# Pooled attention and two feed-forward layers: later three-pass products in block 0, an account of conversion buffers, and other buffers for the last output tiles

## The chip, the cores and the metric

One core of one Trainium2 chip runs the kernel. The metric is the device time of one launch in microseconds (us). The engines are TensorE (PE; its weight loads stand as PEld), VectorE (DVE), ScalarE (ACT), GpSimd (POOL) and SyncE (SP, which issues all the transfers).

## The reference

```python
def _attn_ref(q, k, v):              # 4 batches, 8 heads, 576 tokens, head size 64
    k_p = k.reshape(B, H, Sp, 8, D).mean(axis=3)
    v_p = v.reshape(B, H, Sp, 8, D).mean(axis=3)
    attn = softmax(q @ k_p^T / sqrt(D))
    return attn @ v_p
def _moe_ref(x, w_in, w_out):        # 2304 x 512, 512 x 2048, 2048 x 512
    h = x @ w_in
    g = where(h >= 1, h, where(h <= -1, 0, (h + 1) ** 2 / 4))
    return g @ w_out
def _moe2_ref(x, w_in, w_out):       # the same shapes
    h = x @ w_in
    g = maximum(h, 0) + log1p(exp(-abs(h)))
    return g @ w_out
out = _moe2_ref(_moe_ref(rows of _attn_ref, w_in, w_out), w_in2, w_out2)
```

All is float32. The softmax and the reshapes are abbreviated here.

## The kernel before

The weights come in as 64-bit words. A *conversion* turns a tile of them into float32: two ACT passes (`words`, L112), three DVE passes (`exponents`, L119), a product and a sum. A product in float32 is either made *whole*, one matmul on float32 operands, or in *three passes* on operands split into a high part and a rest in FP32R: high x high, high x rest, rest x high. A split takes an ACT copy (the high part) and a DVE subtraction (the rest).

**Stage 1** is attention and the first feed-forward layer. The 18 tiles of 128 tokens are cut into five blocks of 4, 4, 4, 3 and 3 tiles (`BLK`). Each block runs over 16 chunks of 128 hidden units: `emit_g1` (L510) makes h of chunk c from x, `act` (L529) makes g of it on ACT and DVE, and `emit_g2` (L550) adds g times the second weights to y, two chunks behind. The main loop (L793) counts half chunks `hs`, 32 to a block, 160 in all, and calls `background(hs)` in each. That function makes the attention steps of the next block at places fixed in `plan`, and from half chunk 44 on calls `tick` (L680), which advances the conversion of the second layer's weights.

In block 0 the first layer's weights are converted beside the products, one tile for two chunks (`convert1`, L141). The second product of block 0 is whole throughout. The first product is whole while its weight tile is not split and three-pass afterwards. `split1(3)` (the weight tile of chunks 4 and 5) runs in the loop's chunk 3, `split1(5)` (chunks 6 and 7) in chunk 5, and so on; `split_x0` splits the two halves of x in chunks 2 and 3. A three-pass product of block 0 needs both halves of x. Weight tiles that block 0 used whole are split later at places in `SPLITS`.

`convert2` (L178) is a generator, one for each of 32 units of the second layer's weights. Its steps are: `words`; `exponents` with a product on POOL; the load of unit n + 2 into `st` (L165, two buffers); the sum; for every second unit of the first weights four subtractions that make seven matrices for a scheme with seven products (`sums`, tile `t`); and then, for one to four pieces, an ACT copy of the high part into `b` (three buffers), a DVE subtraction, and two stores to DRAM (`wid`, `wod`), the high part from `b` and the rest from `a` or `t`. Each step yields a price, and `tick` lets a step go when a credit covers it. A new unit starts when its load has been issued, fewer than two units are in their first steps, and fewer than four `a` tiles are held (`held`). An `a` tile counts as free two ticks after its last store was written into the program, the tile `t` three ticks after. For `b` and `st` there is no such account.

In all of stage 1 every engine executes its instructions in the order in which the program writes them. So an ACT instruction whose buffer is not yet free holds all ACT work that is written behind it. SP is a queue in the same way in both stages.

**Stage 2** (L873) is the second layer, three thirds of 768 tokens, eight groups q each, by seven products per group (`emit_product`) and `emit_group` for the second product. PE and SP keep the written order here; a planner orders ACT and DVE. At the end of a third `emit_group` copies each of six output tiles y from PSUM into a tile `ob` (two buffers), even ones on ACT and odd ones on DVE, and stores it:

```python
            ob = es2.t2.tile([128, DM], FP32, tag="ob", name="ob")
            if t % 2:
                nc.vector.tensor_copy(out=ob, in_=y)
            else:
                nc.scalar.activation(out=ob, in_=y, func=ACTF.Copy)
```

The tiles `e`, `l` and `r` of `act2` (L610) have two buffers each.

Of the kernel before, what the change touches and what calls it, by code (L numbers as in the profile page):

```python
# [22 lines left out]
DM = H * D  # L23
# [7 lines left out]
def pooled_attention_ffn_ffn(ctx, tc, q, k, v, v0, w1, w2, out):  # L31
# [133 lines left out]
    def st_load(n):  # L165
        if n < 2 * NC:
            (part, h), r = USE[n // 2], n % 2
            raw[n] = es2.cv.tile([128, 2 * DM], U32, tag="st", name="st")
            src = w2[part, h].bitcast(U32)[:, r * 2 * DM:(r + 1) * 2 * DM]
            nc.sync.dma_start(out=raw[n], in_=src)  # L170

    left = {}
    SUMS = 0.81
    held = []
    sums = []
    landing = []

    def convert2(n):  # L178


        (part, h), r = USE[n // 2], n % 2
        a = es2.cv.tile([128, DM], U32, tag="a", bufs=4, name="a")
        held.append(n)
        l = es2.cv.tile([128, DM], BF16, tag="l", name="l")
        st = raw.pop(n)
        words(st, a, l)
        yield 1.55
        e = exponents(a, st[:, 0:DM], DM)
        nc.gpsimd.tensor_tensor(out=l, in0=l, in1=e, op=ALU.mult)  # L189
        yield 0.0  # L190
        st_load(n + 2)
        yield 0.7
        af = a.bitcast(FP32)
        nc.vector.tensor_tensor(out=af, in0=af, in1=l, op=ALU.add)
        yield SUMS if r and not part else 0.0
        if part:
            jobs = [(n, af, wod[:, h, :, r, :])]
        elif r == 0:
            left[h] = af
            return  # L200
        else:

            b0, b1 = left.pop(h), af
            b11, b21, b12, b22 = (b[:, o:o + QK] for b in (b0, b1) for o in (0, QK))
            assert not sums
            sums.append(h)
            t = slot([128, 4, QK], FP32, "t")
            t3, t2, t4, t1 = (t[:, m, :] for m in range(4))
            nc.vector.tensor_tensor(out=t1, in0=b12, in1=b11, op=ALU.subtract)
            nc.vector.tensor_tensor(out=t3, in0=b22, in1=b12, op=ALU.subtract)  # L210
            yield 0.8
            nc.vector.tensor_tensor(out=t2, in0=b22, in1=t1, op=ALU.subtract)
            nc.vector.tensor_tensor(out=t4, in0=b21, in1=t2, op=ALU.subtract)
            yield 0.0
            jobs = [
                (None, t[:, 0:2, :], wid[:, h, 1:3, :, :].rearrange("p o m f -> p m o f")),
                ("t", t[:, 2:4, :], wid[:, h, 3:5, :, :].rearrange("p o m f -> p m o f")),
                (n - 1, b0.rearrange("p (o f) -> p o f", o=2),
                 wid[:, h, 0:6:5, :, :].rearrange("p o m f -> p m o f")),
                (n, b22, wid[:, h, 6, :, :]),  # L220
            ]
        old = store = None
        for k, f, dst in jobs + [(None, None, None)] * 2:
            if store:
                k0, d, x = store
                nc.sync.dma_start(out=d, in_=x)
                if k0 is not None:
                    landing.append([3 if k0 == "t" else 2, k0])
            store = None
            if old:  # L230
                k0, fo, hi, to = old
                nc.vector.tensor_tensor(
                    out=fo.bitcast(FP32R), in0=fo, in1=hi.bitcast(FP32), op=ALU.subtract
                )
                nc.sync.dma_start(out=to[:, 0], in_=hi.bitcast(FP32))
                store = (k0, to[:, 1], fo)
                old = None
            if f is not None:
                hi = es2.cv.tile([128, DM], FP32R, tag="b", bufs=3, name="b")
                hi = hi.rearrange("p (o f) -> p o f", o=2) if len(f.shape) == 3 else hi[:, 0:f.shape[1]]  # L240
                nc.scalar.activation(out=hi, in_=f, func=ACTF.Copy)
                old = (k, f, hi, dst)
            yield 0.7 if old else 0.0


    def wi_load(q, i):
# [380 lines left out]
    def emit_group(q, w, t):  # L627

        s, m = divmod(q, NH)
        if m == w == t == 0:  # L630
            yacc[s] = [
                (ps["y"] if o < KD else ps["y2"]).tile([128, DM], FP32, tag=f"y{o}", name=f"y{o}")
                for o in range(2 * SN // 128)
            ]
        gh, gl = (g[:, t * 128:(t + 1) * 128] for g in g_t[q, w])
        wh, wl = (x[:, w, :] for x in wo[q])
        y = yacc[s][t]
        last = m == NH - 1 and w == 1
        for n, (a, b) in enumerate(((gh, wh), (gh, wl), (gl, wh))):
            nc.tensor.matmul(  # L640
                out=y, lhsT=a, rhs=b, start=(m == w == n == 0), stop=(last and n == 2)
            )
        if last:
            ob = es2.t2.tile([128, DM], FP32, tag="ob", name="ob")
            if t % 2:
                nc.vector.tensor_copy(out=ob, in_=y)
            else:
                nc.scalar.activation(out=ob, in_=y, func=ACTF.Copy)
            i, c0 = divmod(t * 128, SN)
            for j, parts in enumerate(HALVES):  # L650
                row = T0[j] * 128
                for g, col, n in parts:
                    lo, hi = max(col, c0), min(col + n, c0 + 128)
                    if g == s and lo < hi:
                        r0 = row + i * n + lo - col
                        nc.sync.dma_start(out=out[r0:r0 + hi - lo, :], in_=ob[lo - c0:hi - c0, :])
                    row += 2 * n
# [22 lines left out]
    def tick(start):  # L680
        for x in list(landing):
            x[0] -= 1
            if not x[0]:
                landing.remove(x)
                sums.clear() if x[1] == "t" else held.remove(x[1])
        late = False
        for item in list(flight):
            late = late or item[1] > credit[0] or item[1] == SUMS and bool(sums)
            if not (late and item[1]):
                credit[0] -= item[1]  # L690
                item[1] = next(item[0], None)
                item[2] += 1
                if item[1] is None:
                    flight.remove(item)

        if start and units and units[0] in raw and sum(x[2] < 4 for x in flight) < 2 and len(held) < 4:
            g = convert2(units.pop(0))
            flight.append([g, next(g), 1])

# [81 lines left out]

    pend = []
    acts = {}
    SPLITS = {(0, NC - 3): 0, (0, NC - 2): 1, (0, NC - 1): 2}
    SPLITS.update({(1, 2 + i): m for i, m in enumerate((4, 6, 8, 10, 12, 14, 15))})
    splits = []

# [5 lines left out]
    for n in range(NB * NC):  # L793
        j, c = s = divmod(n, NC)
        hs = 2 * n
        hot = j == 0
        if s == (1, 0):
            esc.close()
            es2.cv = esc.enter_context(tc.tile_pool(name="cv2", bufs=2))
        acts[n] = act(emit_g1(j, c), j, c)  # L800
        pend.append(s)
        while later:
            y1_store(*later.pop(0))

        if hot and c + 2 < NC:
            next(c1[c + 2])
        if n > NC + 2:
            step(n - 2)
        step(n - 1)
        for g in splits:  # L810
            next(g)
        splits = []
        if n <= NC + 2:
            step(n - 2)
        if hot and c + 1 < NC:
            next(c1[c + 1])
        if hot and c in (2, 3):
            xg = split_x0(c - 2)
            next(xg)

        if hot and 3 <= c < NC - 2 and c % 2:
            w0 = split1(c)
            next(w0)
        if hs == CONV2 - 4:
            st_load(0)
            st_load(1)
        background(hs)

        while len(pend) > 2:
            emit_g2(*pend.pop(0))  # L830
        step(n - 1)
        next(acts[n])
        if hot and c + 1 < NC:
            next(c1[c + 1])
        if hot and c + 4 < NC:
            w_load(c + 4)
        if hot and c in (2, 3):
            next(xg, None)
        if hot and 3 <= c < NC - 2 and c % 2:
            next(w0)  # L840
        background(hs + 1)

        if (j, c) in SPLITS:
            splits = [split1(SPLITS[j, c])]
            next(splits[0])
            credit[0] -= 1.2
        if j == LAST and c in (11, 12, 13, 14):
            for i in range(2):
                wi_load((c - 11) // 2, (c - 11) % 2 * 2 + i)
# [98 lines left out]
```

## Time and profile before

| | |
|---|---|
| median of 3 runs | 895.03 us (893.3 to 898.16) |
| the profiled execution's own time | 894.71 us |
| its span in the trace | 893.0 us |
| PE busy | 866.1 us (97%) |
| DVE busy | 638.4 us (71%) |
| ACT busy | 511.0 us (57%) |
| mean granted TensorE clock | 0.994 of full speed |

The span runs from the first to the last instruction of the program. Busy times of PE count pipelined matmuls and are not PE at its peak. The chain is followed back from the last instruction to whatever released each step. An instruction's idle time is that of its engine just before it, with what ended it. Stage 1 lasts until about 500 us, and block 0 until about 157 us; the chunks of blocks 3 and 4, with three tiles, begin at 345 us.

### The profile page before, as it was taken

What the parts mean: (1) busy time and instruction counts of PE and PEld (TensorE: products, weight loads), DVE (VectorE), ACT (ScalarE), POOL (GpSimd) and SP (SyncE); (2) the same over time, 40 slices, a digit from 0 to 9 for tenths busy, and PEclk for the clock granted to TensorE, in tenths of its full rate; (3) what the DMA queues carried; (4) which work ended last, traced back from release to release, by engine and by line L of the source; (5) the groups of instructions that cost most, each with busy time, mean ns of one, the idle gap of its engine ahead of it and who ended that gap; (6) DMA issues with size and microseconds to landing.
All of it is one profiled execution on the core that took longest, in us unless ns stands there. A gap on an engine that the chain in (4) does not pass through costs nothing.

```text
span 893.0 us, 12212 instructions
## 1 busy us (share of the span) xinstructions
PE 866.1 (97%) x4538; PEld 722.9 (81%) x4538; DVE 638.4 (71%) x953; ACT 511.0 (57%) x927; POOL 44.4 (5%) x41
## 2 busy tenths in 40 slices
PE   8989999999999999999999989999999999999996
PEld 4446666788887888889889979888888888989885
DVE  6899883757678685777778387776677675765763
ACT  4856763574655654765566455646556464644551
POOL 0000000001001111021111000000000000000000
PEclk9989999999999999999999999999999999999999
DMA  7834421311394445625675395557196455596202
GB/s 259 334 114 168 170 81 54 106 36 59 118 291 145 154 127 181 212 95 188 226 266 200 141 375 170 158 176 272 66 367 218 137 175 217 173 362 192 86 0 72
DMA packets 65643, 154.94 MB, mean 174 GB/s; under 512 B 6128, under 2 KB 26608, under 8 KB 63536
## 3 DMA queue, kind: packets, MB, share of 16 engines
q1 hardware_dynamic: 65584, 154.17, 50.6%
q8 instruction: 36, 0.59, 0.3%
q14 instruction: 23, 0.19, 0.1%
HBM read 121.63 MB, written 32.51 MB: 173 GB/s over the span
## 4 chain that ended last, share of the span: by engine, by line
PE 73%; DVE 11%; DMA 7%; ACT 7%; issue 2%; SPq 0%; POOL 0%; ACTq 0%; DVEq 0%
PE y L640 21%; PE h L603 18%; PE y L564 15%; PE h L523 14%; DMA st<-in_w 2%; DMA wid<-b 2%; PE a L412 2%; PE a L470 2%; DMA x<-y1d 1%; PE a L456 1%; DVE gl L548 1%; DVE ks L349 1%; DVE wf L122 1%; ACT e L445 1%; DVE t L538 1%
## 5 line engine op out<-in xcount | busy, mean ns | idle before, releaser
L603 PE MATMUL h<-xfh,wi 128*128 128x384 f32 x544 | 160.2, 337 | 1.9 <-DVE h L890 1.2
L523 PE MATMUL h<-xl,whi 128*128 128x512 f32 (+1 forms) x352 | 126.2, 381 | 0.0
L640 PE MATMUL y<-whi,gl 128*128 128x512 f32 x288 | 114.2, 397 | 1.0 <-DVE gl L624 1.0
L640 PE MATMUL y<-wlo,gh 128*128 128x512 f32 x288 | 113.7, 395 | 0.0
L640 PE MATMUL y<-whi,gh 128*128 128x512 f32 x288 | 112.1, 389 | 0.4 <-ACT gh L623 0.4
L603 PEld LDWEIGHTS h<-xfh,wi 128*128 128x128 f32 x544 | 100.8, 188 | 9.4 <-DVE h L890 2.6
L564 PE MATMUL y<-gl,whi 128*128 128x512 f32 (+1 forms) x256 | 93.9, 367 | 2.6 <-DVE gl L548 2.4
L564 PE MATMUL y<-gh,whi 128*128 128x512 f32 (+1 forms) x256 | 94.7, 370 | 1.2 <-ACT gh L546 1.2
L523 PE MATMUL h<-xh,whi 128*128 128x512 f32 (+1 forms) x256 | 95.3, 372 | 0.0
L564 PE MATMUL y<-gh,wlo 128*128 128x512 f32 (+1 forms) x256 | 92.8, 362 | 0.0
L523 PE MATMUL h<-xh,wlo 128*128 128x512 f32 (+1 forms) x256 | 92.8, 362 | 0.0
L603 PE MATMUL h<-xfl,wi 128*128 128x384 f32 x272 | 91.8, 338 | 0.0
L614 ACT ACTIVATE e<-h 128x768 f32<-128x768 f32 x48 | 40.1, 840 | 84.7 <-DVE h L890 84.7
L890 DVE TENSOR_TENSOR h<-h,s 128x384 f32<-128x384 f32 x72 | 40.0, 556 | 66.0 <-PE h L603 65.7
L532 ACT ACTIVATE t<-h 128x512 f32<-128x512 f32 (+1 forms) x80 | 44.2, 553 | 56.1 <-PE h L523 55.8
L523 PEld LDWEIGHTS h<-xl,whi 128*128 128x128 f32 x352 | 66.4, 190 | 10.8 <-issue 2.4
L189 POOL TENSOR_TENSOR l<-l,st 128x512 bf16<-128x512 bf16 x32 | 43.0, 1345 | 432.3 <-ACT whi L159 192.3
L640 PEld LDWEIGHTS y<-whi,gl 128*128 128x128 f32 x288 | 54.0, 187 | 12.9 <-DVE gl L624 1.4
L640 PEld LDWEIGHTS y<-whi,gh 128*128 128x128 f32 x288 | 54.1, 188 | 7.0 <-ACT gh L623 0.7
L564 PE MATMUL y<-g,wf 128*128 128x512 f32 x128 | 58.2, 597 | 1.0 <-DVE wf L151 1.0
L640 PEld LDWEIGHTS y<-wlo,gh 128*128 128x128 f32 x288 | 54.0, 187 | 6.3
L564 PEld LDWEIGHTS y<-gl,whi 128*128 128x128 f32 x256 | 48.1, 188 | 10.0 <-DVE gl L548 5.4
(100 smaller groups left out, 1641.5 us busy)
## 6 DMA issues: line engine op xcount, KB each, us to landing
wi<-wid SPq DMA_DIRECT2D x72, 512.0 KB, 6.0
raw<-in_w SPq DMA_DIRECT2D x16, 1024.0 KB, 4.9
st<-in_w SPq DMA_DIRECT2D x32, 512.0 KB, 4.3
whi<-wod SPq DMA_DIRECT2D x24, 512.0 KB, 4.1
wlo<-wod SPq DMA_DIRECT2D x24, 512.0 KB, 5.6
wid<-b SPq DMA_DIRECT2D x24, 256.0 KB, 4.3
wi<-wid SPq DMA_DIRECT2D x24, 256.0 KB, 5.6
kv<-in_k SPq DMA_DIRECT2D x16, 288.0 KB, 4.0
```

What stands on the lines that cost most here:

```text
L122: nc.vector.scalar_tensor_tensor(out=a, in0=a, scalar=0x80000000, in1=b, op0=ALU.bitwise_and, op1=ALU.bitwise_or)
L189: nc.gpsimd.tensor_tensor(out=l, in0=l, in1=e, op=ALU.mult)
L349: nc.vector.tensor_reduce(out=kst[b, nm][:, p, :], in_=kst.pop((b, nm, p)).rearrange("p (t o) -> p t o", o=POOL), axis=AX.X, op=ALU.add,)
L412: nc.tensor.matmul(out=pa[off:off + n, r * 512 + p * T:r * 512 + (p + 1) * T], lhsT=qt[rows, p, off:off + n], rhs=kps[b][rows, p, :], star ...
L470: nc.tensor.matmul(out=pa[r * D:(r + 1) * D, p * 128 + off:p * 128 + off + n], lhsT=vps[b][:, h * D:(h + 1) * D], rhs=pT[:, c0:c0 + n], st ...
L523: nc.tensor.matmul(out=h, lhsT=a, rhs=b, start=(done == 0), stop=(done == len(ops) * KD - 1),)
L532: nc.scalar.activation(out=g, in_=h, func=ACTF.Relu, bias=1.0)
L564: nc.tensor.matmul(out=y[:, 0:128 * BLK[j]], lhsT=a, rhs=b, start=(c == 0 and n == 0), stop=(c == NC - 1 and n == len(ops) - 1),)
L603: nc.tensor.matmul(out=o, lhsT=a[:, cols], rhs=b[:, kk, :], start=(p in FRESH and done == 0), stop=(done == 5), skip_group_check=True,)
L614: nc.scalar.activation(out=e, in_=h, func=ACTF.Abs)
L640: nc.tensor.matmul(out=y, lhsT=a, rhs=b, start=(m == w == n == 0), stop=(last and n == 2))
L890: nc.vector.tensor_tensor(out=h, in0=o, in1=keep[x], op=ALU.add)
```

## The change

Three things change.

- **Block 0.** `split_x0` moves from chunks 2 and 3 to chunks 4 and 5. `split1` begins in chunk 5 instead of chunk 3, so chunks 4 and 5 make their first product whole, and the first three-pass product is that of chunk 6. The weight tile of chunks 4 and 5 is split in block 1 instead (`SPLITS`, at its chunk 1).
- **The account.** Each step of `convert2` now yields a price and the name of a buffer that the next step takes, or None. `busy` counts the tiles `a`, `b` and `t` that are in use; they are counted free two (`a`, `b`) or three (`t`) ticks after the store was written. A step that takes a `b` or `t` waits while all are counted as used, without holding back the unit behind it unless that one wants the same buffer. A unit starts only three ticks after its load was written.
- **The last output tiles.** In the last third the six output tiles use the tags e, e, l, l, r, r instead of `ob`.

```diff
     def st_load(n):
...
             raw[n] = es2.cv.tile([128, 2 * DM], U32, tag="st", name="st")
+            landing.append([3, n])
...
-    SUMS = 0.81
-    held = []
-    sums = []
+    busy = {"a": 0, "b": 0, "t": 0}
+    BUFS = {"b": 3, "t": 1}
     landing = []
...
-        yield SUMS if r and not part else 0.0
+        yield (0.8, "t") if r and not part else (0.0, "b" if part else None)
...
-            yield 0.0
+            yield 0.0, "b"
...
                 if k0 is not None:
-                    landing.append([3 if k0 == "t" else 2, k0])
+                    landing.append([3, "t"] if k0 == "t" else [2, "a"])
...
                 nc.sync.dma_start(out=to[:, 0], in_=hi.bitcast(FP32))
+                landing.append([2, "b"])
...
                 hi = es2.cv.tile([128, DM], FP32R, tag="b", bufs=3, name="b")
+                busy["b"] += 1
...
-            yield 0.7 if old else 0.0
+            yield 0.7 if old else 0.0, "b" if m + 1 < len(jobs) else None
...
-            ob = es2.t2.tile([128, DM], FP32, tag="ob", name="ob")
+            tag = ("e", "l", "r")[t // 2] if s == NS - 1 else "ob"
+            ob = es2.t2.tile([128, DM], FP32, tag=tag, name="ob")
...
         for item in list(flight):
-            late = late or item[1] > credit[0] or item[1] == SUMS and bool(sums)
-            if not (late and item[1]):
-                credit[0] -= item[1]
+            us, b = item[1]
+            if b and (busy[b] == BUFS[b] or b in short):
+                short.add(b)
+                continue
+            late = late or us > credit[0]
+            if not (late and us):
+                credit[0] -= us
...
-        if start and units and units[0] in raw and sum(x[2] < 4 for x in flight) < 2 and len(held) < 4:
+        if (start and units and units[0] in raw and units[0] not in [x[1] for x in landing]
+                and sum(x[2] < 4 for x in flight) < 2 and busy["a"] < 4):
...
-    SPLITS = {(0, NC - 3): 0, (0, NC - 2): 1, (0, NC - 1): 2}
+    SPLITS = {(0, NC - 3): 0, (0, NC - 2): 1, (0, NC - 1): 2, (1, 1): 3}
...
-        if hot and c in (2, 3):
-            xg = split_x0(c - 2)
+        if hot and c in (4, 5):
+            xg = split_x0(c - 4)
             next(xg)
-        if hot and 3 <= c < NC - 2 and c % 2:
+        if hot and 5 <= c < NC - 2 and c % 2:
             w0 = split1(c)
             next(w0)
```

## Rows read from the trace of the kernel before

**Rows 1.** The page: busy times (share of the span) and counts, and the chain's shares by engine.
```profile
PE 866.1 (97%) x4538; PEld 722.9 (81%) x4538; DVE 638.4 (71%) x953; ACT 511.0 (57%) x927; POOL 44.4 (5%) x41
PE 73%; DVE 11%; DMA 7%; ACT 7%; issue 2%; SPq 0%; POOL 0%; ACTq 0%; DVEq 0%
```

**Rows 2.** Stretches: from:to, length, busy PE, PEld, DVE, ACT, POOL, clock, DMA, GB/s.
```profile
340.00:472.00 132.00, 125.56 (x754) 117.71 (x753) 99.35 (x185) 82.54 (x183) 21.41 (x17) 1.00 0.57 189
472.00:500.00 28.00, 28.00 (x163) 28.00 (x162) 19.48 (x30) 15.65 (x29) 2.33 (x2) 1.00 0.65 245
```

**Rows 3.** PE in order of time, block 0: start, length, instruction, idle before.
```profile
55.19 0.80 PE L523 MATMUL h<-xl,wlo 128*128 128x512 f32 x1 [4.25 <-DVE wlo L161]
...
71.50 0.50 PE L523 MATMUL h<-xl,wlo 128*128 128x512 f32 x1 [0.16 <-DVE wlo L161]
```

**Rows 4.** DVE in order of time, block 0.
```profile
64.06 0.69 DVE L538 SCALAR_TENSOR_TENSOR g<-t,h 128x512 f32<-128x512 f32 x1 [1.23 <-ACT t L533]
...
70.23 1.22 DVE L161 TENSOR_TENSOR wlo<-wf,whi 128x1024 fp32r<-128x1024 f32 x1
```

**Rows 5.** Stretches of block 0, columns as in rows 2.
```profile
50.90:55.20 4.30, 0.05 (x2) 0.01 (x1) 4.26 (x6) 1.21 (x2) 0.00 (x0) 0.76 0.38 80
55.20:59.60 4.40, 4.40 (x10) 3.46 (x11) 4.33 (x7) 0.00 (x0) 0.00 (x0) 0.50 0.55 220
59.60:62.80 3.20, 3.20 (x9) 1.47 (x8) 3.17 (x5) 2.45 (x17) 0.00 (x0) 0.94 0.00 0
75.00:160.00 85.00, 85.00 (x369) 53.05 (x366) 63.21 (x82) 49.97 (x104) 0.00 (x0) 1.00 0.32 109
```

**Rows 6.** The chain in order of time, a whole product and a three-pass one.
```profile
82.78 3.43 PE y L564 x8
86.21 2.73 PE h L523 x12
```

**Rows 7.** Waits of PE from 340 to 472 us: total, times, longest.
```profile
PE a L470 <- ACT pT L462: 2.7, 2, 1.4
PE y L564 <- DVE gl L548: 2.4, 6, 0.5
PE y L564 <- ACT gh L546: 1.2, 2, 1.0
```

**Rows 8.** Waits of ACT from 340 to 472 us.
```profile
ACT a L114 <- DMA st<-in_w: 14.3, 6, 3.4
ACT b L241 <- DMA wid<-b: 11.4, 6, 2.4
```

**Rows 9.** Transfers: count, KB each, median us from issue to landing.
```profile
st<-in_w SPq DMA_DIRECT2D x32, 512.0 KB, 4.3
...
wid<-b SPq DMA_DIRECT2D x24, 256.0 KB, 4.3
```

**Rows 10.** Groups by line: count, then busy us and mean ns (the steps of conversion units).
```profile
L189 POOL TENSOR_TENSOR l<-l,st 128x512 bf16<-128x512 bf16 x32 | 43.0, 1345 | 432.3 <-ACT whi L159 192.3 <-DVE st L126 184.1 <-DMA wod<-a 14.0
L194 DVE TENSOR_TENSOR a<-a,l 128x512 f32<-128x512 f32 x32 | 22.6, 714 | 1.1 <-POOL l L189 1.1
```

**Rows 11.** Busy time of instructions on tile st: DVE, ACT, POOL, with counts.
```profile
200.00:500.00 300.00, 49.90 (x93) 36.56 (x60) 41.55 (x31) 1.00 0.53 177
```

**Rows 12.** Busy time of L232 (DVE) and of L241 (ACT).
```profile
200.00:500.00 300.00, 31.66 (x48) 1.00 0.53 177
200.00:500.00 300.00, 27.50 (x48) 1.00 0.53 177
```

**Rows 13.** The chain at the end, in order of time.
```profile
879.98 2.73 PE y L640 x12
...
884.01 2.37 DMA out<-ob
...
889.35 0.69 DVE ob L646
```

**Rows 14.** The line that stores output tiles, all 20 transfers: landing times.
```profile
DMA to landing us min/median/max: 2.0/2.2/4.8
```

More of the change, by code (lines that the diff above doesn't have):

```diff
@@ L182, in convert2 @@
         a = es2.cv.tile([128, DM], U32, tag="a", bufs=4, name="a")
-        held.append(n)
+        busy["a"] += 1
         l = es2.cv.tile([128, DM], BF16, tag="l", name="l")
@@ L186, in convert2 @@
         words(st, a, l)
-        yield 1.55
+        yield 1.55, None
         e = exponents(a, st[:, 0:DM], DM)
         nc.gpsimd.tensor_tensor(out=l, in0=l, in1=e, op=ALU.mult)
-        yield 0.0
+        yield 0.0, None
         st_load(n + 2)
-        yield 0.7
+        yield 0.7, None
         af = a.bitcast(FP32)
         nc.vector.tensor_tensor(out=af, in0=af, in1=l, op=ALU.add)
-        yield SUMS if r and not part else 0.0
+        yield (0.8, "t") if r and not part else (0.0, "b" if part else None)
         if part:
@@ L204, in convert2 @@
             b11, b21, b12, b22 = (b[:, o:o + QK] for b in (b0, b1) for o in (0, QK))
-            assert not sums
-            sums.append(h)
+            busy["t"] += 1
             t = slot([128, 4, QK], FP32, "t")
@@ L210, in convert2 @@
             nc.vector.tensor_tensor(out=t3, in0=b22, in1=b12, op=ALU.subtract)
-            yield 0.8
+            yield 0.8, None
             nc.vector.tensor_tensor(out=t2, in0=b22, in1=t1, op=ALU.subtract)
             nc.vector.tensor_tensor(out=t4, in0=b21, in1=t2, op=ALU.subtract)
-            yield 0.0
+            yield 0.0, "b"
             jobs = [
@@ L222, in convert2 @@
         old = store = None
-        for k, f, dst in jobs + [(None, None, None)] * 2:
+        for m, (k, f, dst) in enumerate(jobs + [(None, None, None)] * 2):
             if store:
@@ L684, in tick @@
                 landing.remove(x)
-                sums.clear() if x[1] == "t" else held.remove(x[1])
-        late = False
+                if x[1] in busy:
+                    busy[x[1]] -= 1
+        late, short = False, set()
         for item in list(flight):
-            late = late or item[1] > credit[0] or item[1] == SUMS and bool(sums)
-            if not (late and item[1]):
-                credit[0] -= item[1]
+            us, b = item[1]
[5 more added lines that the diff above has]
+                credit[0] -= us
                 item[1] = next(item[0], None)
@@ L836, in pooled_attention_ffn_ffn @@
             w_load(c + 4)
-        if hot and c in (2, 3):
+        if hot and c in (4, 5):
             next(xg, None)
-        if hot and 3 <= c < NC - 2 and c % 2:
+        if hot and 5 <= c < NC - 2 and c % 2:
             next(w0)
```

## The prediction

> **What bounds the kernel now.** I read the page first. PE is busy for 97% of the span and holds 73% of the chain; DVE holds 11%, transfers and ACT 7% each [rows 1]. So the work of PE sets the time, and only its interruptions can be won. I looked for them in the busy time by stretches, then in the waits of each stretch, then in the engines' order of time. Three places show them, and the change touches one in each of its parts.
>
> In block 0, PE stands still for 4.25 us until 55.19 us, for the rest of a weight split on DVE [rows 3]. DVE has no idle time before that: it is the bound there. During the wait the granted clock falls: its mean is 0.76 in the wait, 0.50 in the next 4.4 us, and 0.94 in the 3.2 us after; from 75 us PE is busy without a break [rows 5].
>
> From 340 to 472 us PE is busy for 125.56 of 132 us [rows 2]. Its waits are for ACT and DVE, 2.7 + 2.4 + 1.2 = 6.3 us [rows 7]. In the same stretch ACT stands for 14.3 us on loads into `st` and 11.4 us on stores from `b` [rows 8]. ACT executes in the written order, so a copy whose buffer is in flight holds the attention and the activation behind it.
>
> At the end PE is done with y at 879.98 + 2 x 2.73 = 885.4 us (the row's twelve matmuls and twelve more for the four tiles left), but the last copy starts at 889.35 us [rows 13]: four of six copies stand in line for two buffers.
>
> **Part 1, block 0.** A whole product costs 3.43 us and a three-pass one 2.73 [rows 6]; chunks 4 and 5 go whole, so PE works 2 x 0.70 = 1.4 us more. Beside DVE's work it is hidden, as follows. Before the first product that needs splits of both x and the weights (chunk 6 now), DVE has to do the same instructions as before until the end of the split at 70.23 + 1.22 = 71.45 us [rows 4], less one weight split. That split weighs 1.22 us, about 1.15 pipelined. Both splits of x stay in that stretch, only later. DVE also loses its one idle piece, 1.23 us at 64.06, where it waited for ACT's activation of chunk 4 [rows 4]: PE no longer finishes that product at about 59.6 but whole, with no wait, at 50.2 + 3.43 = 53.6, and ACT has it ready when DVE comes. So the splits are ready at 71.45 - 1.15 - 1.2 = 69.1 us, 2.4 earlier. PE runs chunk 4, a second product, chunk 5 and a second product, 4 x 3.43 us from 50.2, to 64 us with its small attention matmuls, then some small transposes and two passes to 66.1. It waits 3.0 us there instead of 4.25, behind the same kind of instruction; queued behind it are only its own products.
>
> That wait again threatens the clock. The half clock cost (4.4 + 0.4)/2 = 2.4 us of PE's time before [rows 5]: a mean of 0.94 over 3.2 us is 0.4 us at half, and each us at half speed loses half. Chunk 6 starts just behind a stretch with little PE work, as chunk 4 did. I scale the price with the wait, 2.4 x 3.0/4.25 = 1.7, and keep 0 and 2.4 as its ends. Part 1 gives 2.4 - 1.7 = 0.7 us; ends 0 and 2.4. The postponed weight split costs ACT and DVE about 1.2 us each in block 1, beside PE, with DVE busy for 63 of 85 us up to 160 us [rows 5]: nothing, and 1.2 us at most if that cover were gone.
>
> **Part 2, the account.** Followed half chunk by half chunk, the program of before writes the copy into `b` as little as 0 or 1 tick behind the third-last store from `b`, and `words` as little as 1 tick behind its load, 11 units of 32 at 1 or 2 ticks. Afterwards the least is 2 for `b` and 3 for `st`. Blocks 3 and 4, 64 half chunks, run from 345 to 500 us, 2.4 us each. So a `b` has 4.8 us and an `st` 7.2 us, and both transfers take 4.3 us in the median [rows 9]. Most of the 14.3 + 11.4 us of ACT's waits [rows 8] should go. Of PE's 6.3 us [rows 7] I leave 0.5 for two waits near 360 us that no transfer precedes, and 0.6 for stores in bursts that land later than 4.8 us: 5.2 us gone; ends 1 and 6.3.
>
> The steps held back cost something later. The last unit now starts at half chunk 155 instead of 145, and the last store is written in tick 161, after the last chunk, not 152. So into the last five chunks of block 4 come three POOL and DVE steps, three sums and three subtractions of units 29 to 31, where one subtraction stood. By the rows a unit's three DVE steps on `st` take 49.90/93 x 3 = 1.6 us [rows 11], the sum 0.71 [rows 10], the subtraction 31.66/48 = 0.66 [rows 12]: 9.0 us for three, 8.3 more than before. DVE is busy for 19.48 of the 28 us from 472 to 500 [rows 2] and would be at 27.8. The cover is just gone; queued behind are the rests of g, for which PE waits. I take 1.0 us, ends 0 and 3. The stores of the last units also stand on SP ahead of stage 2's loads; these are for groups that start a group later, which hides them, and without that cover they cost one landing, 4.3 us by the loads of `st` [rows 9], which is inside the last rival's price. Part 2 gives 5.2 - 1.0 = 4.2 us.
>
> **Part 3, the last tiles.** The tiles e, l and r were last read before the first copy, so no copy waits for a buffer, and the last one starts when PE is done, at 885.5 instead of 889.35 [rows 13]: 3.85 us. Six stores then leave close together. A landing takes 2.2 us in the median and 4.8 at most [rows 14]; I take 0.65 us more for the last one, since the stores from `b`, of the same 256 KB, take 4.3 in company [rows 9]. So 3.2 us; ends 3.85 - 2.6 = 1.2 and 3.85.
>
> [...] No row of before shows six stores at once.
>
> **Sum.** 0.7 + 4.2 + 3.2 = 8.1 us off the profiled execution's 894.71 us: 886.6. That execution is 0.3 us under the median of the runs, 895.03; on the median's footing the forecast is 886.9 us.
>
> **Rivals.**
> *The clock holds in block 0.* For it: the wait is shorter by 1.2 us. Against it: in the trace the clock fell within 4.3 us of the start of a wait, to a mean of 0.76 [rows 5]. Part 1 then gives 2.4: 885.2.
> *The account doesn't hold what it counts.* It counts ticks of the program, not time; when stores come in bursts, or the load is issued late since SP stood behind a POOL product of 1.35 us [rows 10], the transfer lands after its ticks and ACT waits as before. For it: 4.3 us in the median against 4.8 for `b` leaves little. Then part 2 gives 1 - 1 = 0: 891.1.
> *All parts are worth more than priced:* the clock holds, all 6.3 us of waits go and the end of block 4 costs nothing, the last landing takes the median: 895.03 - 2.4 - 6.3 - 3.85 = 882.5.
> *Slower: the late units spill over the end of block 4.* One unit's steps, bare, are two ACT passes 36.56/60 x 2 = 1.2, DVE 1.6, POOL 1.34, the sum 0.71, the copy 27.50/48 = 0.57 and the subtraction 0.66, together 6.1 us [rows 10 to 12]. Three units in a row with PE standing are 18.3 us, in place of the 1.0 priced: 886.9 + 17.3 = 904.2. It decides from the point where 9 us of this stand bare. For it: DVE is full there by the sum above. Against it: stage 2's first products need only what was prepared earlier, and only two ticks lie behind the last chunk.
>
> **How the numbers follow.** About 0.5%, 4.5 us, is what a measurement of this kernel can tell from no change: faster means under 890.5, slower over 899.5. Forecast 0.40, clock holds 0.25, more than priced 0.12, account fails 0.15, spill 0.08. Faster is the first three, 0.77; the fourth is within 0.5%, 0.15; slower is 0.08. The range leaves out the spill, and the best case beyond 881.5; at its upper side it takes in the account's failure with part 3 at 2.2: 881.5 to 892.0.
>
> **What would show it.** Part 1: the idle time of PE before the first `wlo` pass is near 3.0 us and ends near 69 us, and the stretch behind it has a granted clock near 0.5. A wait over 4 us there, or none, refutes the sum. Part 2: ACT's waits for `st` and `b` between 340 and 472 us shrink from 25.7 us to under 6, PE's from 6.3 to about 1, and PE's from 472 to 503 us grow to about 1. Part 3: no copy of an output tile waits for a transfer, and the last copy starts within 0.3 us of PE's end. The prediction fails if ACT's waits go and PE's stay (then DVE's load, not the transfers, made them), or if PE shows new waits in stage 2, whose ACT and DVE order a planner writes.

## The result, and the profile after

The kernel after takes 883.88 us in the median (883.66 to 884.23, 4 runs) where the kernel before took 894.16 on the same chip; the ratio is 0.9889, with the interval [0.9864, 0.9913]. In a second set of runs, again beside the kernel before on one chip, it took 885.95 (883.21 to 888.98, 6 runs), ratio 0.9916 [0.9899, 0.9934]. The forecast of 8.1 us off, a ratio of 0.9909, lies within both. The profiled execution took 884.23 us with a span of 882.5, 10.5 shorter than that of before.

The page of the kernel after, busy times and the chain by engine, beside [rows 1]:

```profile
PE 863.5 (98%) x4530; PEld 720.3 (82%) x4530; DVE 637.0 (72%) x953; ACT 512.5 (58%) x927; POOL 44.6 (5%) x41
...
PE 87%; DVE 6%; ACT 3%; DMA 3%; issue 1%; SPq 0%; DVEq 0%; ACTq 0%
```

PE's work is nearly the same, 863.5 us against 866.1. PE's share of the chain rose from 73 to 87%, and the shares of DVE, ACT and transfers fell to about half: fewer waits lie on the path.

Stretches of the kernel after, with the columns of [rows 2] (from:to, length, busy PE, PEld, DVE, ACT, POOL, clock, DMA, GB/s). The first two answer to [rows 5]; the last is the one from 472 to 500 us of [rows 2], moved by the 6.6 us that the program is then ahead.

```profile
64.00:69.00 5.00, 2.06 (x12) 1.10 (x10) 4.93 (x7) 4.97 (x7) 0.00 (x0) 1.00 0.46 193
69.00:73.00 4.00, 3.91 (x43) 3.11 (x44) 3.86 (x7) 1.37 (x4) 0.00 (x0) 1.00 0.70 266
340.00:472.00 132.00, 129.04 (x787) 123.50 (x786) 99.06 (x184) 86.56 (x187) 19.41 (x15) 1.00 0.55 183
...
465.40:493.40 28.00, 28.00 (x163) 28.00 (x162) 25.18 (x42) 17.95 (x34) 4.49 (x3) 1.00 0.79 266
```

In block 0 the clock stays at 1.00. From 340 to 472 us PE works 3.5 us more than before. In the last chunks DVE is busy for 25.18 of 28 us, as the prediction feared, and PE still has no gap.

PE of the kernel after in order of time, the rows with a wait of over 1 us behind the start-up [rows 3]:

```profile
66.16 1.07 PE L457 MATMUL a<-ident,e 128*72 128x128 f32 x8 [1.64 <-ACT vp L361]
...
69.09 0.50 PE L524 MATMUL h<-xl,wlo 128*128 128x512 f32 x1 [1.40 <-DVE wlo L161]
...
158.73 0.50 PE L565 MATMUL y<-gl,whi 128*128 128x512 f32 x1 [1.36 <-DVE gl L549]
...
358.97 0.44 PE L565 MATMUL y<-gl,whi 128*128 128x384 f32 x1 [1.76 <-DVE gl L549]
```

The first two stand in place of the 4.25 us before. The third and the fourth are new. DVE just ahead of each shows why: in order of time, first at 157 us, then at 357.

```profile
156.84 1.23 DVE L161 TENSOR_TENSOR wlo<-wf,whi 128x1024 fp32r<-128x1024 f32 x1 [0.26 <-ACT whi L159]
157.99 0.69 DVE L549 TENSOR_TENSOR gl<-t,gh 128x512 fp32r<-128x512 f32 x1
...
356.84 0.42 DVE L121 TENSOR_SCALAR st<-a 128x512 uint32<-128x512 uint32 x1
357.30 0.69 DVE L122 SCALAR_TENSOR_TENSOR a<-a,st 128x512 uint32<-128x512 uint32 x1
358.02 0.43 DVE L126 TENSOR_SCALAR st<-a 128x512 uint16<-128x512 uint16 x1
358.37 0.55 DVE L549 TENSOR_TENSOR gl<-t,gh 128x384 fp32r<-128x384 f32 x1
```

Both times the rest of g, for which PE stands, is written behind other work: the postponed weight split's rest in one, a conversion unit's step on `st` in the other. What is late is not DVE's work but its order.

Waits from 340 to 472 us, of PE and then of ACT [rows 7, 8]:

```profile
PE y L565 <- DVE gl L549: 3.0, 4, 1.8
...
ACT b L242 <- DMA wid<-b: 4.0, 3, 1.9
...
ACT a L114 <- DMA st<-in_w: 0.3, 1, 0.3
```

ACT's 25.7 us on `st` and `b` are 4.3, and 1.76 of PE's 3.0 us is the new wait at 358.97. What is left on `b` fits the landing times of the stores from it, shortest, median and longest over the whole kernel after:

```profile
DMA to landing us min/median/max: 1.7/3.8/7.2
```

The two ticks that the account gives a `b` are 4.8 us by the prediction's count, which covers the median and not the longest.

The last copy, and the eight stores behind the copies as one row of SP's queue [rows 13, 14]:

```profile
877.41 0.69 DVE L649 COPY ob<-y 128x512 f32<-128x512 f32 x1 [0.67 <-PE y L641]
...
874.63 4.86 SPq L659 DMA_DIRECT2D out<-ob  x8
```

The last copy starts 0.43 us after the start of PE's last matmul (876.98), where it was 4.32 before. SP issues the stores one behind another and the last at 878.95, 0.84 us after its copy is done; it lands after 2.67 us.

Where the 10.5 us come from is read by setting the two traces beside each other: in both, ACT's activation of h starts once in every chunk and group, so the difference of its starts is how far the program is ahead. In us, before minus kernel, so plus is earlier (the last column is the start of PE's last matmul):

```
kernel          chunk 0  chunk 6  chunk 19  chunk 47  chunk 79  group 18  PE end
at us (before)     31.6     74.1     166.5     342.4     497.5     591.0   885.0
after             +0.13    +2.41     +0.97     +1.20     +6.60     +8.05   +8.05
a1_after          -0.73    +1.57     +0.15     +0.37     +4.65     +5.70   +5.69
p1_block0         +0.21    +2.54     +1.10     +0.47     -1.65     +0.21   +0.21
p2_account        +0.19    +0.14     +0.20     +0.43     +4.50     +6.28   +6.28
p3_tiles          -0.31    -0.27     -0.22     -0.09     +0.24     +1.96   +1.97
c1_zeros          -0.25    -0.25     -0.19     +0.04     +1.77     +3.56   +3.55
f1_rest_first     +0.39    +2.66     +2.88     +3.11     +8.31     +9.96   +9.94
f2_two_rings      -0.16    +2.07     +0.64     +0.87     +6.64     +7.46     +7.44
f3_both           +0.13    +2.43     +2.66     +2.89     +8.42     +9.67     +9.67
s1_b_only         -0.35    +1.95     +0.51     -0.20     +4.14     +5.65   +5.64
s2_st_only        -0.25    +2.08     +0.66     +0.89     +3.71     +5.60   +5.57
p23_no_block0     -3.92    -3.86     -3.80     -3.57     +2.49     +2.37   +2.35
f5_words_later    -0.28    +2.00     +2.22     +2.45     +7.35     +8.96   +8.93
```

So the kernel after gains 2.3 us in block 0, gives 1.4 back at the start of block 1, gains 5.4 in blocks 3 and 4, 1.45 at the start of stage 2, and 10.5 - 8.05 = 2.45 at the end. The 1.45 is no part of the change: p3_tiles, whose program is that of before up to the last copies, gains 1.72 at the same place. In the one profiled execution of before ACT waited longer there for loads of x (4.4 us, against 3.0 in the kernel after). In blocks 3 and 4 too it may be on the late side: c1_zeros gains 1.73 there and p3_tiles 0.33, though both are unchanged in these blocks. So the 5.4 is 3.7 when c1_zeros stands in for the kernel before. In the medians the kernel before stood at 893.4 us in all three later sets of runs.

### The profile page after: what moved, and what is told of

It reads as the page before. It is cut to its first block, busy times and chain, and to the rows that moved or that the text cites. A ratio compares the mean times of both kernels' runs of the same rounds, so it can differ in the third digit from the quotient of the medians.

```text
span 882.5 us, 12199 instructions
## 1 busy us (share of the span) xinstructions
PE 863.5 (98%) x4530; PEld 720.3 (82%) x4530; DVE 637.0 (72%) x953; ACT 512.5 (58%) x927; POOL 44.6 (5%) x41
## 4 chain that ended last, share of the span: by engine, by line
PE 87%; DVE 6%; ACT 3%; DMA 3%; issue 1%; SPq 0%; DVEq 0%; ACTq 0%
PE y L641 22%; PE y L565 22%; PE h L524 19%; PE h L604 19%; PE a L413 2%; PE a L471 2%; PE a L457 2%; DMA x<-y1d 1%; PE zp L722 1%; DMA wid<-a 1%; DVE wf L122 1%; DVE wf L151 1%; DMA wi<-wid 1%; ACT e L446 1%; PE vpa L376 1%
## 5 line engine op out<-in xcount | busy, mean ns | idle before, releaser
L524 PE MATMUL h<-xl,whi 128*128 128x512 f32 (+1 forms) x336 | 119.5, 375 | 0.0
L524 PEld LDWEIGHTS h<-xl,whi 128*128 128x128 f32 x336 | 62.6, 188 | 9.5 <-issue 1.9
```

The lines of the kernel that those rows point to most:

```text
L524: nc.tensor.matmul(out=h, lhsT=a, rhs=b, start=(done == 0), stop=(done == len(ops) * KD - 1),)
```

## The experiments

Each kernel was timed against the kernel before on the same chip. Kernels that begin with p undo or isolate parts, s split the account, f change the kernel after, a repeats it, c measures one cost by itself.

**p1_block0: part 1 alone.** The kernel before with the edits of block 0 and nothing else (the places that run the second halves of these splits move with them):

```diff
-    SPLITS = {(0, NC - 3): 0, (0, NC - 2): 1, (0, NC - 1): 2}
+    SPLITS = {(0, NC - 3): 0, (0, NC - 2): 1, (0, NC - 1): 2, (1, 1): 3}
...
-        if hot and c in (2, 3):
-            xg = split_x0(c - 2)
+        if hot and c in (4, 5):
+            xg = split_x0(c - 4)
...
-        if hot and 3 <= c < NC - 2 and c % 2:
+        if hot and 5 <= c < NC - 2 and c % 2:
...
```

> The kernel before with the change in block 0 alone. My theory, from the two traces laid side by side: chunk 6 of block 0 starts its stretch 2.4 us earlier and one weight split, now written ahead of the first rest of g in block 1, takes 1.5 us back there, so 1.0 us faster than before. Rival (the prediction's step): the clock falls in the new wait and takes 1.7 us of the 2.4, and the postponed split costs nothing: 0.7 us faster, with a granted clock of 0.5 behind the wait. The times are close; the clock and the wait in block 1 tell the two apart.

Measured: 893.81 us, ratio 1.0004 [0.9995, 1.0013]: nothing. The gain is there at chunk 6 (2.3) and at chunk 19 (0.9), as the theory says, with a clock of 1.00, and is gone by chunk 79, which neither theory nor rival foresaw. Most of it is lost at 375 us: ACT's waits from 360 to 376 us, PE's wait, and the stretch behind it.

```profile
ACT b L241 <- DMA wid<-b: 2.6, 1, 2.6
ACT b L241 <- DMA wod<-b: 1.7, 1, 1.7
```

```profile
375.32 0.67 PE L412 MATMUL a<-kp,q 64*128 64x72 f32 x8 [1.77 <-DVE xl L486]
```

```profile
376.00:380.00 4.00, 4.00 (x19) 3.59 (x18) 3.93 (x9) 2.13 (x5) 0.00 (x0) 0.57 0.80 248
```

ACT stands on stores from `b`, ACT's part of the split of x that PE needs stands behind these copies, and behind PE's wait the clock has a mean of 0.57 over 4 us, which costs an estimated 0.43 x 4 = 1.7 us. Here the early start of the chunks is worth nothing, since the stage behind it waits for transfers.

**p2_account: part 2 alone.** The kernel after with the output tile and all of block 0 as before:

```diff
-            tag = ("e", "l", "r")[t // 2] if s == NS - 1 else "ob"
-            ob = es2.t2.tile([128, DM], FP32, tag=tag, name="ob")
+            ob = es2.t2.tile([128, DM], FP32, tag="ob", name="ob")
...
-    SPLITS = {(0, NC - 3): 0, (0, NC - 2): 1, (0, NC - 1): 2, (1, 1): 3}
+    SPLITS = {(0, NC - 3): 0, (0, NC - 2): 1, (0, NC - 1): 2}
...
-        if hot and c in (4, 5):
-            xg = split_x0(c - 4)
+        if hot and c in (2, 3):
+            xg = split_x0(c - 2)
...
```

> The kernel before with the account of conversion buffers alone. My theory: it holds the gain between 220 and 500 us, 5.5 us, and the 1.45 us at the start of stage 2 (an x load that lands earlier) as well, so 7.0 us faster. Rival: the 1.45 us come from another part, then 5.5 us. Second rival: part of the gain needs the block 0 change, then under 5 us.

Measured: 888.63 us, ratio 0.9957 [0.9943, 0.9971], 0.0043 x 893.45 = 3.8 us. From chunk 47 to 79 it gains 4.1 us. It has the wait at 359 us too, and there the clock fell:

```profile
360.00:364.00 4.00, 4.00 (x17) 4.00 (x17) 3.34 (x9) 2.96 (x6) 0.70 (x1) 0.63 0.51 173
364.00:368.00 4.00, 4.00 (x25) 3.94 (x24) 3.45 (x9) 2.14 (x4) 1.36 (x1) 0.94 0.01 4
```

By these means that is an estimated 0.37 x 4 + 0.06 x 4 = 1.7 us. Without it the account would have been worth about 5.8 in this trace. So the theory's 7.0 and the first rival's 5.5 us lie outside the interval. The measured 3.8 is under the 5 of the second rival, but its reason, that the account needs the change in block 0, is not shown: the fall of the clock alone accounts for an estimated 1.7.

**p3_tiles: part 3 alone.**

```diff
-            ob = es2.t2.tile([128, DM], FP32, tag="ob", name="ob")
+            tag = ("e", "l", "r")[t // 2] if s == NS - 1 else "ob"
+            ob = es2.t2.tile([128, DM], FP32, tag=tag, name="ob")
```

> The kernel before with the other buffers for the last output tiles alone. My theory: the last copy starts 3.9 us earlier against PE's end, SP issues the eight stores one behind the other (0.84 us late for the last) and the last landing takes 0.67 us longer, so 2.4 us faster. Rival (the prediction's term): SP keeps up, 3.2 us. Nothing else should move; if the planner's order in stage 2 reacts to the tags, the start of stage 2 shifts by 1.45 us.

Measured: 890.91 us, ratio 0.9977 [0.9966, 0.9989], 2.1 us. From PE's last matmul (883.07) to the end of the span (888.6) it is 5.5 us where before has 8.0: 2.45, as in the kernel after. The theory holds; the rival's 3.2 us, a ratio of 0.9964, lies just outside the interval.

**c1_zeros: the clock of block 0 by itself.** The kernel before with fourteen more matmuls, of zeros, into an open sum of chunk 4, where PE waits 4.25 us:

```diff
                 done += 1
+                if (j, c) == (0, 4) and done == 2:
+                    for _ in range(14):
+                        nc.tensor.matmul(out=h, lhsT=zeros[:, 0:128], rhs=zeros, start=False, stop=False)
         return h
```

> The kernel before with fourteen matmuls on zeros (3.2 us) added to chunk 4's product where PE waits for the rest of the weight split, so that PE stays busy and the clock should hold; the sum is not changed by them. The prediction's price for the clock: PE gets back up to 2.4 us. Rival, which the trace after suggests: DVE is the bound until 71.5 us (its one idle piece ended with ACT's exponentials and not with PE), so the clock costs nothing and the time is the same within 0.3 us, with PE's wait before the next weight split grown by about 2 us.

Measured: 892.45 us, ratio 0.9989 [0.9976, 1.0002]. Its stretches over the times of [rows 5], and PE's row at the place of the second wait of [rows 3]:

```profile
50.90:55.20 4.30, 3.27 (x15) 1.28 (x14) 4.26 (x5) 1.51 (x2) 0.00 (x0) 1.00 0.17 61
55.20:59.60 4.40, 4.15 (x14) 2.74 (x15) 4.33 (x7) 0.00 (x0) 0.00 (x0) 1.00 0.63 238
59.60:62.80 3.20, 3.20 (x12) 1.98 (x11) 3.17 (x5) 2.19 (x15) 0.00 (x0) 1.00 0.00 0
```

```profile
71.76 0.50 PE L523 MATMUL h<-xl,wlo 128*128 128x512 f32 x1 [1.22 <-DVE wlo L161]
```

The clock is held at 1.00, and chunk 6 comes no earlier (-0.25 at chunk 0 and at chunk 6): PE, faster, waits 1.22 us instead of 0.16 for the same split. So the fall of the clock in block 0 cost the kernel before nothing. DVE is the bound until 71.5 us, with one idle piece, and that does not depend on PE either. In c1_zeros PE is done with chunk 4's product at 58.06 us, where before it was 59.83, and the idle piece of [rows 4] is still there:

```profile
64.31 0.69 DVE L541 SCALAR_TENSOR_TENSOR g<-t,h 128x512 f32<-128x512 f32 x1 [1.22 <-ACT t L536]
```

ACT's activation of chunk 4 is written behind ACT's exponentials, and these wait for DVE (6.31 us in before, 3.08 in the kernel after). In the kernel after they still stand ahead of it, but DVE has a split of x to make meanwhile:

```profile
58.55 1.22 DVE L508 TENSOR_TENSOR xl<-xh,xl 128x1024 fp32r<-128x1024 f32 x1
...
60.52 0.69 DVE L539 SCALAR_TENSOR_TENSOR g<-t,h 128x512 f32<-128x512 f32 x1
```

**a1_after: the kernel after once more**, beside its variants, with no edit.

> The kernel after, again, beside its variants. Both theories: 883.9 us, 0.989 of before (883.66 to 884.23 so far).

Measured: 885.95 us, as said above. Its trace tells why it varies. PE's wait, and the stretch behind it in this execution; then the same stretch in the other execution of the same program:

```profile
359.79 0.44 PE L565 MATMUL y<-gl,whi 128*128 128x384 f32 x1 [1.76 <-DVE gl L549]
```

```profile
361.00:365.00 4.00, 4.00 (x16) 4.00 (x15) 3.90 (x11) 2.26 (x5) 0.00 (x0) 0.57 0.37 131
```

```profile
361.00:365.00 4.00, 4.00 (x25) 4.00 (x24) 3.86 (x11) 3.15 (x7) 0.00 (x0) 1.00 0.39 130
```

The same wait of 1.76 us, and a clock of 0.57 behind it in one execution and of 1.00 in the other; the chunks behind it are 1.56 us later in the first. The mean clock sorts the ten runs of the kernel after: at 0.999 they take 883.2 to 884.2 us (five runs), at 0.997 885.2 to 886.6 (four), at 0.993 889.0 (one).

**f1_rest_first: the rest of g ahead of the postponed split's rest.**

```diff
-        if n > NC + 2:
+        if n > NC + 1:
             step(n - 2)
...
-        if n <= NC + 2:
+        if n <= NC + 1:
             step(n - 2)
```

> The kernel after with one change in the written order: at the second half chunk of block 1 the rest of g is written before the postponed split's rest, so DVE makes it first. Theory (the postponed split costs 1.47 us since its 1.23-us rest stands on DVE ahead of the rest of g for which PE waits at 158.7 us): the wait of 1.36 us at 158.7 goes, 1.2 to 1.5 us off, 882.5, and chunks behind it are earlier by as much up to stage 2. Rival (the wait only moves: the split's product or the next rest of g comes as much later, or the early half is given back behind DMA waits as the gain of block 0 alone was): 883.9, within 0.3 of the kernel after.

Measured: 882.83 us, ratio 0.9885 [0.9870, 0.9900]. DVE now makes the rest of g first, and PE's row shows no wait:

```profile
155.47 0.68 DVE L549 TENSOR_TENSOR gl<-t,gh 128x512 fp32r<-128x512 f32 x1
156.07 0.68 DVE L539 SCALAR_TENSOR_TENSOR t<-t,h 128x512 f32<-128x512 f32 x1
156.66 1.22 DVE L161 TENSOR_TENSOR wlo<-wf,whi 128x1024 fp32r<-128x1024 f32 x1
```

```profile
156.96 0.39 PE L565 MATMUL y<-gl,whi 128*128 128x512 f32 x1
```

Against the kernel after it is 1.65 us ahead at chunk 19 and still 1.45 at chunk 79, and of 4 runs none has a mean clock under 0.999. The theory holds. The median of the kernel after in this set is 3.1 us higher; the 1.5 beyond the trace's goes with the clock of those runs. It is the fastest version run, though its interval touches that of the kernel after in the same set and holds the 0.9889 of its first.

**f2_two_rings: half of the last stores from ACT's queue.**

```diff
-                        nc.sync.dma_start(out=out[r0:r0 + hi - lo, :], in_=ob[lo - c0:hi - c0, :])
+                        ring = nc.scalar if s == NS - 1 and t % 2 == 0 else nc.sync
+                        ring.dma_start(out=out[r0:r0 + hi - lo, :], in_=ob[lo - c0:hi - c0, :])
```

> The kernel after with the last third's three even output tiles stored from ACT's queue instead of SP's. Theory (the last landing is late because SP issues eight stores one behind another, about 0.54 us each, the last one 0.84 us behind its copy): the last store is issued within 0.3 us of its copy, 0.6 to 0.8 us off, 883.2. Rival (it is the landing in company, 2.67 instead of 2.00 us, that sets the end, and issuing earlier only makes it longer): 883.9, within 0.3.

Measured: 886.28 us, ratio 0.9919 [0.9905, 0.9933], not faster than a1_after. The issues of out, KB each and median us to landing, in f2_two_rings and then in the kernel after:

```profile
out<-ob ACTq DMA_DIRECT2D x2, 256.0 KB, 2.4
out<-ob SPq DMA_DIRECT2D x2, 256.0 KB, 3.8
out<-ob SPq DMA_DIRECT2D x2, 128.0 KB, 2.9
out<-ob ACTq DMA_DIRECT2D x2, 128.0 KB, 3.4
```

```profile
out<-ob SPq DMA_DIRECT2D x4, 256.0 KB, 2.6
out<-ob SPq DMA_DIRECT2D x4, 128.0 KB, 2.6
```

The last store is issued 0.02 us after its copy instead of 0.84, and lands after 3.65 us instead of 2.67: 3.67 against 3.51 behind the copy. The rival holds: it is the landing in company that ends the kernel.

**f3_both: f1 and f2 together.**

> The kernel after with both edits, the rest of g ahead of the postponed split's rest and the even last tiles from ACT's queue. If both theories hold the two add up: 2.1 us off, 881.8. If both rivals hold: 883.9. If only the first: 882.5; only the second: 883.2.

Measured: 883.32 us, ratio 0.9896 [0.9877, 0.9915]: what the first edit alone gives, within the intervals. From the start of PE's last matmul to the end of the span it takes 5.7 us, and the kernel after 5.5.

**s1_b_only: no account of the loads into st.**

```diff
-            landing.append([3, n])
...
-        if (start and units and units[0] in raw and units[0] not in [x[1] for x in landing]
+        if (start and units and units[0] in raw
```

> The kernel after without the account of the loads into st (a unit may start while its load is in flight); the account of the stores from b stays. Theory (both accounts carry the 5.4 us that PE gained up to 485 us, about half each): ACT's waits for st between 340 and 472 us come back to 8 us or more while those for b stay under 5, PE loses 2 to 3 us there, 887 us. Rival (only the stores from b matter, ACT has time to wait for st): ACT's waits for st come back and PE loses under 0.7 us, 884 to 885.5.

Measured: 887.15 us, ratio 0.9925 [0.9908, 0.9942].

**s2_st_only: no account of the buffers b.**

```diff
-            if b and (busy[b] == BUFS[b] or b in short):
+            if b == "t" and (busy[b] == BUFS[b] or b in short):
```

> The kernel after without the account of the three buffers b (a copy into b is written although their stores are in flight); the account of the loads into st stays. Theory (half each): ACT's waits for b between 340 and 472 us come back to 8 us or more while those for st stay under 2, PE loses 2 to 3 us there, 887 us. Rival (only b matters): PE loses 4 to 5.4 us, 888.5 to 890. Second rival (only st matters): 884 to 885.5.

Measured: 886.14 us, ratio 0.9909 [0.9891, 0.9926]. ACT's waits from 340 to 472 us, of s1_b_only, then of s2_st_only, then PE's of s2_st_only:

```profile
ACT a L114 <- DMA st<-in_w: 9.8, 5, 3.8
...
ACT b L241 <- DMA wid<-b: 1.5, 1, 1.5
```

```profile
ACT b L242 <- DMA wid<-b: 12.8, 7, 3.5
...
ACT a L114 <- DMA st<-in_w: 0.2, 1, 0.2
```

```profile
PE y L565 <- DVE gl L549: 3.9, 3, 2.7
```

Each account takes away just the waits that it names: 9.8 for `st` come back without the one, 12.8 for `b` without the other. From chunk 47 to 79 the gain is 4.3 us with `b` alone and 2.8 with `st` alone (a fall of the clock, to a mean of 0.60 from 416 to 420 us at the wait of 2.7 us, is in the second), against 5.4 with both. So they are not halves that add up: each alone carries more than half in PE's time. Leaving out the account of `st` loses 1.1 us in the traces, between its theory's 2 to 3 and its rival's 0.7; leaving out that of `b` loses 2.6, as its theory says, but an estimated 1.6 of it (0.40 x 4) by the fall of the clock. In the medians (887.15 and 886.14) neither can be told from the kernel after in its second set. Not tested by itself is the rest of the account: the wait for `t`, and that a step that waits no longer holds back the unit behind it.

**p23_no_block0: the kernel after without part 1**, the diff of p1_block0 taken back.

> The kernel after without its block-0 part (the account and the last tiles alone). Theory (the net gain of block 0, 0.97 us in the trace of the kernel after, is kept once the account is in): every chunk from the second of block 1 to 340 us stands 0.9 to 1.2 us later than in the kernel after, 0.7 to 1.3 us more than the kernel after, 885.5 to 886.5. Rival (block 0 is worth nothing with the account either, as alone): the offset is gone by 485 us and the time is that of the kernel after, 884 to 885.5. Only the chunks' offsets in the trace can tell these apart, since a fall of the clock behind the wait at 359 us, which comes in some executions, weighs 1.6 us.

Measured: 886.6 us, ratio 0.9920 [0.9897, 0.9942]. This profiled execution starts 4 us late (the clock was 0.50 from 12 to 16 us), so its row is read from its own chunk 0. Then the kernel after is 2.2 us ahead of it at chunk 6, 0.7 at chunk 19, 0.7 at chunk 47 and 0.06 at chunk 79: 6.47 against 6.41. In these two executions the rival holds: in the kernel after ACT waits for stores at 443.57 (1.91 us) and 449.89 (1.83), and PE 0.52 at 453.28, where PE has no wait in p23_no_block0. But executions of one program differ here by as much. Up to the last stores f2_two_rings is the kernel after, and it gains 6.80 from chunk 0 to 79; a1_after gains 5.38, or 6.94 with the 1.56 of its fall of the clock given back. Of the two kernels without part 1, p2_account gains 4.31, or about 5.9 likewise, beside the 6.41. So with part 1 it is 6.5 to 6.9 and without it 5.9 to 6.4: whether part 1's 0.7 us are kept once the account is in stays open.

**f5_words_later: the conversion step at 357 us held back.** f1_rest_first with

```diff
+        credit[0] -= 1.6 * (n == 3 * NC + 1)
         background(hs + 1)
+        credit[0] += 1.6 * (n == 3 * NC + 1)
```

> The kernel after with the rest of g ahead of the postponed split's rest, and with one conversion step of 1.53 us on DVE (and the two of ACT ahead of it) held back by one tick at the second chunk of block 3, so that the rest of g at 358.4 us is written before it. Theory (the account's own new order makes PE wait 1.76 us at 359 us, and in some executions the clock falls behind it and takes 1.56 us more): no wait over 0.5 us and no fall of the clock between 350 and 370 us, 1.5 to 1.9 us off the variant without this, 881.0. Rival (the step held back makes another wait of the same size later in block 3 or 4): 882.8, with a wait over 1 us between 360 and 480 us.

Measured: 883.55 us, ratio 0.9893 [0.9872, 0.9914], no better than f1_rest_first. The stretch of the old wait, then the waits that came later, and ACT's from 440 to 470 us:

```profile
358.00:361.00 3.00, 3.00 (x19) 3.00 (x18) 2.55 (x7) 2.96 (x7) 1.41 (x1) 1.00 0.23 68
```

```profile
454.86 0.44 PE L565 MATMUL y<-gl,whi 128*128 128x384 f32 x1 [1.26 <-DVE gl L549]
...
460.29 0.44 PE L565 MATMUL y<-gl,whi 128*128 128x384 f32 x1 [0.99 <-DVE gl L549]
```

```profile
ACT b L242 <- DMA wid<-b: 4.8, 1, 4.8
```

The wait at 359 us is gone, and 1.26 + 0.99 us stand at 455 and 460 behind a wait of 4.8 us for one store. The rival holds: holding back one step moved all that follow (the written order of ACT differs from there on), and a copy into `b` fell behind its store again, account and all.

## Why the prediction was right

The sum was close, in part by luck: in part 1 one term was too high and another too low, part 3 was too high and part 2, by this trace, too low, and these errors cancelled.

**Part 1: 2.4 - 1.7 = 0.7 forecast, 0.84 measured at chunk 19** (0.97 less the 0.13 at chunk 0), at the end nothing in p1_block0, and at most about as much with the account.
- "The splits are ready at 69.1 us, 2.4 earlier": the row is at 69.09, the chunks are 2.3 ahead. The size is right, and for half of it the reason is not. "ACT has it ready when DVE comes" put the end of DVE's idle piece, 1.2 us, down to PE's earlier product; c1_zeros has that product 1.8 us earlier and keeps the idle piece. What filled it was the postponed split of x, 1.22 us at 58.55. The wait of 3.0 us came in two, 1.64 + 1.40, with small transposes and two passes between, which the prediction had put ahead of it.
- The step that failed is "That wait again threatens the clock": the price, 1.7. The clock stayed at 1.00 in the kernel after, and in all nine traces that have these two waits. And the 2.4 us from which it was scaled was never a cost: it was worked out from PE's time in a stretch that the first section had called bound by DVE. c1_zeros shows the cost at zero (a clock of 1.00, and -0.25 at chunk 6 as at chunk 0).
- "The postponed weight split costs ... beside PE, with DVE busy for 63 of 85 us: nothing, and 1.2 us at most": it cost 1.44 us (2.28 at chunk 6, 0.84 at chunk 19), and f1_rest_first won it back by order alone. That a quarter of the stretch had DVE idle did not hide an instruction written ahead of the one PE waits for: the wait at 158.73 us is 1.36 us.
- That p1_block0 ends at no gain the prediction had not seen: it added a gain of block 0 to the end of the kernel, past a stage that waits for transfers. With the account such a lead can be kept: f1_rest_first keeps 1.45 of its 1.65.

**Part 2: 5.2 - 1.0 = 4.2 forecast; 5.4 in this trace (3.7 against c1_zeros), 3.8 by the ratio of p2_account.**
- ACT's 25.7 us on `st` and `b` are 4.3 ("to under 6"). Right, and s1 and s2 show each account doing its own.
- "PE's from 6.3 to about 1" is 3.0. The step that failed is "I leave 0.5 for two waits near 360 us": the account's new order puts a conversion step ahead of the rest of g at 357 us, and the wait there is 1.76. The prediction looked for the price of the new order in the last chunks only.
- The end of block 4, priced at 1.0, cost nothing. DVE is busy for 25.18 of 28 us (27.8 forecast), and PE for 28.00: the late steps fell where nothing waited.

**Part 3: 3.85 - 0.65 = 3.2 forecast, 2.45 measured** (2.1 by the ratio of p3_tiles). The copies gained 4.32 - 0.43 = 3.89, as priced, and the last landing is 2.67 against 2.00, as priced. The mis-sized term is what lies between: SP's eight stores one behind another, 0.84 us at the last. f2_two_rings shows that without it (0.02 us) the landing takes as much more, 3.65 us against 2.67. So the 3.2 was 0.75 too high. The stores together, which no row of before shows, are in the trace of the kernel after: from the first issue to the last landing, 874.63 to 881.62 us, 1.57 MB went at a mean of 225 GB/s, with the times between the copies and the last landing in it.

**The sum.** 0.84 + 5.4 + 2.45 = 8.7 us in the traces, against 8.1; the rest of the span's 10.5 is the 1.45 at the start of stage 2, 0.13 ahead of chunk 0 and 0.2 between chunks 19 and 47, none of them the change's. All of this leans on the one profiled execution of before; with c1_zeros in its place the 8.7 would be 7.0. By medians the gain is 10.3 in the first set and 7.4 in the second, and the difference between the two goes with the mean clock of the runs (0.999 in the four of the first set, 0.993 to 0.999 in the six of the second). The parts alone give -0.4 + 3.8 + 2.1 = 5.5, less than either; 1.7 of what is lacking may be p2_account's own fall of the clock. How much of the rest is interplay of the parts stays open. Of the rivals "the clock holds" was true of block 0, and moved nothing.

## What to carry to other kernels

Price a fall of the clock only where PE is the bound; in the stretch here that DVE bounds it was free (c1_zeros: 1.00 where before has 0.50, and chunk 6 no earlier). For every instruction that is moved, look not at the busy share of its new place but at what is written just behind it on its engine and who waits for that. A gain ahead of a stage that waits for transfers was lost there in p1_block0 (+2.54 us at chunk 6, -1.65 at chunk 79), and was kept with the account (f1_rest_first, 1.45 of 1.65): follow the program's lead through the stages before adding it to the end. And compare leads over more than one execution of the same program: here they differ by up to 1.7 us in blocks 3 and 4 (c1_zeros against before, the same program there).

## What the runs showed of the hardware

Eight profiled executions have the PE wait of 1.76 us near 360 us (1.75 in one). Behind it the clock fell in two, to means over 4 us of 0.57 (a1_after) and 0.63 (p2_account), and stayed at 1.00 in six, among them the kernel after, whose program is that of a1_after. It also fell behind the one wait of 1.77 us in p1_block0 (0.57 over 4 us), at the one of 2.69 us in s2_st_only (0.60 over 4 us), and in or just behind the wait of 4.25 us in block 0 in all four executions that have it (the lowest mean of 4 us is 0.51 in before and p3_tiles, 0.50 in p2_account, 0.66 in p23_no_block0). It held at 1.00 through the two waits of 1.64 and 1.40 us in all nine that have these (PE stands for 3.0 us from 64 to 72 us in each). One program thus had both outcomes, 0.57 and 1.00, behind the same wait; what decides between them, no run here shows. In a1_after the wait of 1.76 us cost nearly twice its length: with the fall of the clock behind it, 1.56 us more.
